# Half of the second Gram matrix taken in plain fp32 in the opening, with the opening's order and two bank queues changed

## The chip, the cores and the metric

The kernel runs on one NeuronCore of a Trainium2 chip. The metric is the time of one execution in microseconds (us). Before the change three runs gave 2222.56, 2222.73 and 2224.01 us, with 2222.73 as the median. One execution of the kernel was also profiled. All durations and waits below come from that trace.

The core's engines are called by the profile's names: PE (TensorE) multiplies matrices, ACT (ScalarE), DVE (VectorE) and POOL (GpSimd) do element-wise work, and SP issues the DMA transfers. Each engine works through its own queue in order, and they wait for each other by semaphores.

## What is computed

```python
def _attn_ref(q, k, v, tau):            # (4, 6080, 256) each
    qn = q / (norm(q, axis=1) + 1e-6);  kn = k / (norm(k, axis=1) + 1e-6)
    s = kn.transpose(0, 2, 1) @ qn / tau            # 256 x 256 per batch
    a = exp(s - s.max(-1));  a /= a.sum(-1) + 1e-9
    return v @ a
def _moe_ref(x, w_in, w_out):           # x: the 24320 rows of v @ a
    h = x @ w_in                                    # 2048 wide
    g = where(h >= 1, h, where(h <= -1, 0, (h + 1)**2 / 4))
    return g @ w_out
```

## The kernel before

**Per batch.** The Gram matrix k^T q (256 x 256) and the column norms give the softmax matrix. The kernel never forms v @ a: it multiplies the softmax matrix into each 256-wide slice of w_in (`make_W`) and applies the result to v.

**Groups.** The main loop runs over 192 groups: 4 batches, 6 column pairs of the transposed v (five of 2 x 512 columns, one of 2 x 480) and 8 slices. A group's 2 x 2 block product is done with seven block products instead of eight (Strassen's scheme in Winograd's form): `make_V` prepares the seven combinations of v (`V_T1` to `V_T4`, `V_11`, `V_21`, `V_22`) once per pair, `make_W` those of the weights. `h_ops` issues the seven products. They run through PSUM bank A (bank_119 in the order's rows), one of two Z banks (bank_125 or bank_126) and bank B (bank_120): products `S1*V_T1`, then `A11*V_11` (Z), `S2*V_T2` (Z), `A12*V_21` (A), `S3*V_T3` (Z), `S4*V_22` (B), `A22*V_T4` (Z). ACT and DVE copy and add between banks in between (L615, L617, L620, L624). `tile_ops` turns the four blocks of h into g (L589 to L599), and `o_ops` multiplies by w_out into four banks O00 to O11 (bank_121 to bank_124).

**Number format.** Each product of this kind is three fp32r matmuls (`mm3`, L378) on a value split into a high part and a remainder: high x high, high x remainder, remainder x high. A value is split by a cast (on ACT, or for two of the four g blocks on DVE, by `CAST_ON_DVE`) and a subtraction on DVE. The weights w_in and w_out arrive as float64 words and are converted by seven DVE instructions and two ACT instructions each (`convert`, L331 to L347).

**Gram matrices.** Batch 0's is done in the opening in plain fp32 from 1 MB chunks of k and q (L691), in four slots of memory that the g and v buffers take over afterwards; there ACT squares and DVE adds the squares for the norms (L682, L684). Batches 1 to 3 have theirs done during the groups of the batch before, in 24 chunks of 256 rows each (`gram_chunk`): a load, an ACT cast (L387), a DVE subtraction (L388), 12 matmuls (L378, `kqs`), and a DVE addition (L405).

**What sets the order.** Every operation is recorded with an engine, an estimated duration, a due number and its buffers. `Order.run` places them one after the other: on each engine, of what could start by its own clock, the one that starts first, and among those that could start now the one with the smallest due number. The order of placing is the order of each engine's queue on the chip; at run time only semaphores hold an instruction. A buffer pool gives a slot to whichever operation asks first, unless it is `ordered`. Bank A and bank B are pools of one slot each, so two groups that compete for bank A are served in the order in which the planner placed them.

## Time and profile before

| | us |
|---|---|
| three runs: median (lowest, highest) | 2222.73 (2222.56, 2224.01) |
| profiled execution | 2220.52 |
| its span, first to last instruction | 2218.7 |
| PE busy | 2168.8 |
| DVE busy | 1755.6 |
| ACT busy | 1655.3 |
| POOL busy | 219.2 |

The span is 1.8 us shorter than the execution it belongs to, and that execution is 2.2 us below the median of the runs. A row of the stretch view gives, for a stretch of the span, each engine's busy time with the number of instructions, then the clock granted to PE (1.00 is full speed), the share of the DMA engines' time in use, and GB/s. A row of the time line gives start, duration, engine, line, operation, operands, count of merged instructions, and in brackets the idle time before it and what ended it.

### The profile page before, as it was taken

How to read it: one execution, taken by the hardware profiler on the slowest of the kernel's cores; microseconds unless marked ns; L12 is line 12 of the kernel's file. 1: busy time of each engine (PE TensorE's matmuls, PEld its weight loads, DVE VectorE, ACT ScalarE, POOL GpSimd, SP SyncE). 2: the span in 40 equal slices, each digit the busy share in tenths (PEclk: the TensorE clock that was granted, in tenths of full speed). 3: DMA queues.
4: the chain of work that ended last, by engine and by line, in shares of the span. 5: the costliest groups of instructions: out<-in, count | busy, mean ns of one | idle time of the engine just before them, and what ended most of it. 6: DMA issues, size and time to landing. Idle time of an engine off the chain costs nothing.

```text
span 2218.7 us, 28354 instructions
## 1 busy us (share of the span) xinstructions
PE 2168.8 (98%) x10122; PEld 1818.8 (82%) x10122; DVE 1755.6 (79%) x2844; ACT 1655.3 (75%) x2964; POOL 219.2 (10%) x236
## 2 busy tenths in 40 slices
PE   8698999999999999999999999999999999999998
PEld 6476888888888888888888888888888888888887
DVE  7896778778878787877878888788787777778776
ACT  6576777777777777777778778787777777677775
POOL 1220000001012000010012100000002201000000
PEclk9799999999999999999999999999999999999999
DMA  8463444543435445445334554454442423333331
GB/s 329 164 223 111 171 178 143 193 159 136 150 124 203 172 145 187 156 152 196 114 112 177 185 187 145 160 197 146 165 148 90 175 102 115 126 104 118 120 119 35
DMA packets 84207, 340.16 MB, mean 153 GB/s; under 512 B 8800, under 2 KB 12896, under 8 KB 82656
## 3 DMA queue, kind: packets, MB, share of 16 engines
q1 hardware_dynamic: 84064, 338.33, 42.9%
q8 instruction: 80, 1.31, 0.2%
q14 instruction: 63, 0.52, 0.1%
HBM read 279.84 MB, written 58.46 MB: 152 GB/s over the span
## 4 chain that ended last, share of the span: by engine, by line
PE 91%; ACT 1%; DVE 1%; DMA 0%; issue 0%; POOL 0%; SPq 0%; ACTq 0%; POOLq 0%; DVEq 0%
PE bank L378 91%; ACT u L589 0%; DMA raw<-vT 0%; ACT u L591 0%; DVE u L593 0%; DVE x L599 0%; DVE w_mem L513 0%; ACT bank L617 0%; ACT mh_mem L615 0%; DVE bank L620 0%; DMA outT<-y_mem 0%; ACT v L552 0%; POOL sf_mem L510 0%; ACT x L598 0%; DVE mh_mem L624 0%
## 5 line engine op out<-in xcount | busy, mean ns | idle before, releaser
L378 PE MATMUL bank<-x,wout 128*128 128x512 f32 (+1 forms) x3972 | 1019.6, 389 | 2.3 <-DVE x L599 2.0
L378 PE MATMUL bank<-v,w_mem 128*128 128x512 f32 (+1 forms) x3264 | 850.7, 390 | 15.7 <-ACT bank L617 5.8
L378 PEld LDWEIGHTS bank<-x,wout 128*128 128x128 f32 x3972 | 741.4, 188 | 148.7 <-DVE x L599 5.1
L378 PEld LDWEIGHTS bank<-v,w_mem 128*128 128x128 f32 x3264 | 611.6, 189 | 147.5 <-ACT bank L617 8.9
L589 ACT ACTIVATE u<-bank 128x512 f32<-128x512 f32 (+1 forms) x576 | 342.1, 594 | 311.1 <-PE bank L378 300.4
L593 DVE TENSOR_TENSOR u<-bank,u 128x512 f32<-128x512 f32 (+1 forms) x576 | 391.7, 680 | 138.9 <-ACT u L591 138.6
L599 DVE TENSOR_TENSOR x<-u,x 128x512 fp32r<-128x512 f32 (+1 forms) x662 | 452.4, 691 | 28.4 <-ACT x L598 22.6
L591 ACT ACTIVATE u<-u 128x512 f32<-128x512 f32 (+1 forms) x768 | 468.0, 625 | 5.3
L598 ACT CAST x<-u 128x512 fp32r<-128x512 f32 (+1 forms) x331 | 202.6, 612 | 30.5 <-DVE u L593 27.8
L378 PE MATMUL bank<-x,w_mem 128*128 128x512 f32 (+1 forms) x768 | 208.6, 389 | 0.8 <-ACT bank L617 0.7
L620 DVE TENSOR_TENSOR bank<-bank,mh_mem 128x512 f32<-128x512 f32 (+1 forms) x192 | 133.0, 693 | 74.8 <-PE bank L378 73.3
L378 PE MATMUL bank<-g,wout 128*128 128x512 f32 (+1 forms) x636 | 177.7, 388 | 0.0
L593 DVE TENSOR_TENSOR u<-mh_mem,u 128x512 f32<-128x512 f32 (+1 forms) x192 | 135.6, 706 | 45.7 <-ACT u L591 45.6
L378 PEld LDWEIGHTS bank<-x,w_mem 128*128 128x128 f32 x768 | 143.8, 188 | 30.7 <-ACT bank L617 1.1
L624 DVE TENSOR_TENSOR mh_mem<-bank,mh_mem 128x512 f32<-128x512 f32 (+1 forms) x192 | 131.3, 684 | 39.9 <-PE bank L378 36.2
L615 ACT COPY mh_mem<-bank 128x512 f32<-128x512 f32 (+1 forms) x192 | 111.6, 581 | 51.3 <-PE bank L378 43.1
L596 DVE CAST x<-u 128x512 fp32r<-128x512 f32 (+1 forms) x331 | 141.5, 428 | 8.1
L378 PEld LDWEIGHTS bank<-g,wout 128*128 128x128 f32 x636 | 118.8, 188 | 23.7 <-DVE g L599 0.4
L617 ACT COPY bank<-bank 128x512 f32<-128x512 f32 (+1 forms) x192 | 109.9, 572 | 31.3 <-PE bank L378 22.0
L546 POOL TENSOR_TENSOR t<-raw,raw 128x512 f32<-128x512 f32 (+1 forms) x24 | 35.1, 1464 | 924.9 <-DMA raw<-vT 606.3
L589 ACT ACTIVATE u<-mh_mem 128x512 f32<-128x512 f32 (+1 forms) x192 | 119.2, 621 | 9.2 <-DVE mh_mem L624 8.6
L378 PEld LDWEIGHTS bank<-kqs 128*128 128x128 f32 (+1 forms) x864 | 113.2, 191 | 5.6
(83 smaller groups left out, 1491.8 us busy)
## 6 DMA issues: line engine op xcount, KB each, us to landing
w_mem<-w_d SPq DMA_DIRECT2D x160, 896.0 KB, 4.6
raw<-kq SPq DMA_DIRECT2D x69, 512.0 KB, 5.4
raw<-kqT SPq DMA_DIRECT2D x60, 512.0 KB, 6.1
w_d<-w_mem SPq DMA_DIRECT2D x32, 896.0 KB, 4.5
raw<-vT SPq DMA_DIRECT2D x40, 512.0 KB, 6.4
outT<-y_mem SPq DMA_DIRECT2D x80, 256.0 KB, 2.2
win<-win_d SPq DMA_DIRECT2D x24, 512.0 KB, 3.9
kq<-kq SPq DMA_DIRECT2D x11, 1024.0 KB, 8.3
```

What stands on the lines that cost most here:

```text
L378: nc.tensor.matmul(out, lhsT=lhs(a), rhs=rhs(c), start=start and m == 0, stop=stop and m == 2, skip_group_check=skip)
L546: op("POOL", pool_us(n), lambda: nc.gpsimd.tensor_tensor(out=tt(x), in0=a(), in1=c(), op=ALU.subtract), r=r, w=[ts[x]], due=due + d, gates ...
L589: op("ACT", act_us(n), lambda: nc.scalar.activation(us(), src(), IDENTITY_SAT240, scale=240.0), r=[h], w=[u], due=d_sat)
L591: op("ACT", act_us(n), lambda: nc.scalar.activation(us(), us(), AF.Square, bias=0.5, scale=1.0 / 480.0), w=[u], due=d_sq)
L593: op("DVE", dve_us(n), lambda: nc.vector.tensor_tensor(out=us(), in0=src(), in1=us(), op=ALU.max), r=[h], w=[u], due=d_max)
L596: op("DVE", dve1_us(n), lambda: nc.vector.tensor_copy(t.ap[:, 0, :n], us()), r=[u], w=[t], due=d_hi)
L598: op("ACT", act_us(n), lambda: nc.scalar.copy(t.ap[:, 0, :n], us()), r=[u], w=[t], due=d_hi)
L599: op("DVE", dve_us(n), lambda: nc.vector.tensor_tensor(out=t.ap[:, 1, :n], in0=us(), in1=f32(t.ap[:, 0, :n]), op=ALU.subtract), r=[u], w=[ ...
L615: op("ACT", act_us(n), lambda: nc.scalar.copy(m5.ap[:, :n], a.ap[:, :n]), r=[a], w=[m5], due=d - U)
L617: op("ACT", act_us(n), lambda: nc.scalar.copy(a.ap[:, :n], z.ap[:, :n]), r=[z], w=[a], due=d - U)
L620: op("DVE", dve_us(n), lambda: nc.vector.tensor_tensor(out=bb.ap[:, :n], in0=z.ap[:, :n], in1=m5.ap[:, :n], op=ALU.add), r=[z, m5], w=[bb] ...
L624: op("DVE", dve_us(n), lambda: nc.vector.tensor_tensor(out=h22.ap[:, :n], in0=z.ap[:, :n], in1=m5.ap[:, :n], op=ALU.add), r=[z, m5], w=[h2 ...
```

## The change

What it does, part by part:

- **Batch 1's first 3072 rows** (`EARLY` = 6 chunks of 512) are loaded into the opening's four slots behind batch 0's, and multiplied in plain fp32 into bank O11 (bank_124), with due number 8; DVE copies the sum once into batch 1's accumulator (L743). The 12 `gram_chunk` calls for these rows go. The other 12 are spread over groups 6 to 40 of batch 0 instead of 2 to 40. The squares for batch 1's norms are still all made during batch 0's groups.
- **The opening's order.** Due numbers for the opening are written as times; the softmax of batch 0 and the first `make_W` are `URGENT`, and an urgent operation may be preferred though it is up to `SOON` = 0.6 us from being ready. All eight w_out conversions are placed by the table at the end of the diff. The fold of the two halves of the squares (L701) is done by PE as a second matmul for each norm; the single matmul that writes bank B once (L699) moves behind the norms. The negated row maximum is made for each half of the softmax separately.
- **The first group's weights**: the four sums of `make_W` on DVE instead of POOL, and the split in two parts of three and four products. The order of the weights' parts is permuted.
- **Banks A and B** are ordered pools: groups get them in the order of their numbers.
- **Casts** of g blocks from group 8 on, and of v from the third column pair on, may go to ACT or DVE, whichever the planner finds first; in groups 0 to 7 all go to ACT.
- The planner's estimates of POOL's durations and of DMA bandwidth are changed.

```diff
+URGENT = -1000.0
+SOON = 0.6
...
-    BYTES = 350e3
+    BYTES = 380e3
...
-    def op(self, eng, dur, fn, r=(), w=(), due=0.0, gates=(), size=0):
+    def op(self, eng, dur, fn, r=(), w=(), due=0.0, gates=(), size=0, other=None):
...
+        o.alts = {eng: (dur, fn)}
+        if other:
+            o.alts[other[0]] = other[1:]
...
-                    if best is not None and t > now and t >= best[0][0]:
+                    t = base[o.n, e]
+                    if best is not None and t > now + SOON and t >= best[0][0]:
...
-                    key = (now, o.due, o.n) if t <= now else (t, o.due, o.n)
+                    key = (now, o.due, o.n) if t <= now or o.due <= URGENT and t <= now + SOON else (t, o.due, o.n)
                     if best is None or key < best[0]:
-                        best = (key, o)
+                        best = (key, o, e)
...
-            (t, _, _), o = pick
-            avail[o.eng].remove(o)
+            (t, _, _), o, o.eng = pick
+            t = max([t, base[o.n, o.eng]] + [self.slot(b, o.eng)[0] for b in o.bufs if b.ap is None])
+            o.dur, o.fn = o.alts[o.eng]
...
-A11, A12, A22, S1, S2, S3, S4, A21 = range(8)
+    return 0.35 + 0.0021 * n
...
+S1, A11, S2, A12, S3, S4, A22, A21 = range(8)
...
-CAST_ON_DVE = {(1, 0), (1, 1)}
...
+EARLY = 6
+FIRST = 8
...
     for i, n in enumerate(("A", "B", "O00", "O01", "O10", "O11")):
-        pools[n] = Pool([banks[i]])
+        pools[n] = Pool([banks[i]], ordered=n in ("A", "B"))
...
-        op("DVE", 0.1, lambda: V.tensor_scalar(out=nmax(), in0=nmax(), scalar1=-1.0, scalar2=None, op0=ALU.mult),
-           w=[c], due=due + 6)
+            op("DVE", 0.1, lambda it=it: V.tensor_scalar(out=nmax()[:, it:it + 1], in0=nmax()[:, it:it + 1],
+                                                        scalar1=-1.0, scalar2=None, op0=ALU.mult), w=[c],
+               due=due + 4 + it)
...
+    def make_W(b, i, due, gates=(), parts=((0, NS),), eng="POOL"):
...
-            op("POOL", pool_us(128), lambda d=d, a=a, c=c, o=o: nc.gpsimd.tensor_tensor(
+            v = {"POOL": nc.gpsimd, "DVE": nc.vector}[eng]
+            op(eng, pool_us(128) if eng == "POOL" else dve_us(128), lambda d=d, a=a, c=c, o=o, v=v: v.tensor_tensor(
                 out=f.ap[:, d, :], in0=f.ap[:, a, :], in1=f.ap[:, c, :], op=o), w=[f], due=due + 3)
-        op("ACT", act_us(NS * P), lambda: nc.scalar.copy(w.ap[:, 0], f.ap[:, :NS, :]), r=[f], w=[w], due=due + 5)
-        op("DVE", dve_us(NS * P), lambda: nc.vector.tensor_tensor(
-            out=w.ap[:, 1], in0=f.ap[:, :NS, :], in1=f32(w.ap[:, 0]), op=ALU.subtract), r=[f], w=[w], due=due + 7)
+        for j0, j1 in parts:
+            js, n = slice(j0, j1), (j1 - j0) * P
+            op("ACT", act_us(n), lambda js=js: nc.scalar.copy(w.ap[:, 0, js], f.ap[:, js, :]), r=[f], w=[w],
+               due=due + 5)
+            op("DVE", dve_us(n), lambda js=js: nc.vector.tensor_tensor(
+                out=w.ap[:, 1, js], in0=f.ap[:, js, :], in1=f32(w.ap[:, 0, js]), op=ALU.subtract), r=[f], w=[w],
+               due=due + 7)
...
             op("ACT", act_us(n), lambda: nc.scalar.copy(vs[x].ap[:, 0, :n], get()), r=r, w=[vs[x]], due=due + d,
-               gates=gates)
+               gates=gates, other=("DVE", dve1_us(n), lambda: nc.vector.tensor_copy(vs[x].ap[:, 0, :n], get()))
+               if (b, k) > (0, 1) else None)
...
-        if (x, y) in CAST_ON_DVE:
-            op("DVE", dve1_us(n), lambda: nc.vector.tensor_copy(t.ap[:, 0, :n], us()), r=[u], w=[t], due=d_hi)
-        else:
-            op("ACT", act_us(n), lambda: nc.scalar.copy(t.ap[:, 0, :n], us()), r=[u], w=[t], due=d_hi)
+        op("ACT", act_us(n), lambda: nc.scalar.copy(t.ap[:, 0, :n], us()), r=[u], w=[t], due=d_hi,
+           other=("DVE", dve1_us(n), lambda: nc.vector.tensor_copy(t.ap[:, 0, :n], us())) if g >= FIRST else None)
...
-    S = -120.0
+    T0 = 58.0
+    at = lambda us: (us - T0) / 0.65
...
+    n0 = len(big)
+    big += [(1, i * 512, P, 4) for i in range(EARLY)]
+    st.g = buf("Z")
+    g1 = buf("O11")
+    acc = Buf(acc_early)
...
+    def big_chunk(i, b, r0, p, T):
+        rb, g = Buf(kq_early), (st.g, g1)[b]
+        due = at(3.6 * i + 4) if b == 0 else 8.0
+        kq_ops.append(load(rb, lambda: kq[b, r0:r0 + p * T].rearrange("(p t) s c -> p (t s c)", t=T),
+                           lambda: rb.ap[:p, :T * 512], due - 25 if b == 0 else at(56), p * T * 2048,
+                           [kq_ops[n0 - 1]] if b else ()))
+        last = i == (n0 if b == 0 else len(big)) - 1
+        for t in range(T):
+            def mm(t=t):
+                for it in range(CT):
+                    k0 = t * 512 + it * P
+                    nc.tensor.matmul(g.ap[:, it * C:(it + 1) * C], lhsT=rb.ap[:p, k0:k0 + P],
+                                     rhs=rb.ap[:p, t * 512 + C:t * 512 + 2 * C], start=(r0 == 0 and t == 0 and it == 0),
+                                     stop=(last and t == T - 1 and it == CT - 1), skip_group_check=True)
+            op("PE", CT * 0.433, mm, r=[rb], w=[g], due=due)
+        if b:
+            return
...
-        def mm(rb=rb, p=p, T=T, i=i):
-            for t in range(T):
-                for it in range(CT):
-                    k0 = t * 512 + it * P
-                    nc.tensor.matmul(st.g.ap[:, it * C:(it + 1) * C], lhsT=rb.ap[:p, k0:k0 + P],
-                                     rhs=rb.ap[:p, t * 512 + C:t * 512 + 2 * C],
-                                     start=(i == 0 and t == 0 and it == 0),
-                                     stop=(i == len(big) - 1 and t == T - 1 and it == CT - 1), skip_group_check=True)
-        op("PE", T * CT * 0.45, mm, r=[rb], w=[st.g], due=due)
...
-            op("PE", 1.0, lambda rb=rb: nc.tensor.matmul(banks[1], lhsT=ident, rhs=rb.ap[:, :TB], start=True, stop=True),
-               r=[rb], w=[buf("B")], due=due)
-    op("DVE", dve_us(512), lambda: nc.vector.tensor_tensor(out=accv()[:, :512], in0=accv()[:, :512],
-                                                          in1=accv()[:, 512:1024], op=ALU.add), w=[acc0], due=-60)
...
     def norm_sums():
         for j in range(2 * CT):
-            nc.tensor.matmul(st.pt.ap[:, j:j + 1], lhsT=accv()[:, j * P:(j + 1) * P], rhs=ones[:, 0:1], start=True,
-                             stop=True)
-    op("PE", 1.0, norm_sums, r=[acc0], w=[st.pt], due=-60)
-    softmax(0, -50)
-    for i, due in enumerate((-110, -60, -30)):
-        make_w_in(i, due, [kq_ops[min(2 + 4 * i, 12)]])
-    for i, due in enumerate((-80, -50, -20, -10, 0)):
-        make_w_out(i, due, [kq_ops[min(5 + 4 * i, 12)]])
-    make_V(0, 0, -40, [kq_ops[9]], 1.0)
+            for h in range(2):
+                nc.tensor.matmul(st.pt.ap[:, j:j + 1], lhsT=acc.ap[:, h * 512 + j * P:h * 512 + (j + 1) * P],
+                                 rhs=ones[:, 0:1], start=(h == 0), stop=(h == 1))
+    def mark_b():
+        nc.tensor.matmul(banks[1], lhsT=ident, rhs=acc.ap[:, :TB], start=True, stop=True)
+    for i, x in enumerate(big):
+        big_chunk(i, *x)
+    st.pt = buf("Z")
+    op("PE", 1.4, norm_sums, r=[acc], w=[st.pt], due=URGENT - 20)
+    op("PE", 0.9, mark_b, r=[acc], w=[buf("B")], due=at(56))
+    softmax(0, URGENT - 20)
+    sts[1].g = buf("gacc")
+    op("DVE", dve_us(512), lambda: nc.vector.tensor_copy(sts[1].g.ap.rearrange("p i c -> p (i c)"), g1.ap), r=[g1],
+       w=[sts[1].g], due=10.0)
+    for kind, i, due, gate_ in (("in", 0, 14, 1), ("out", 0, 26, 3), ("in", 1, 34, 5), ("v", 0, 38, 7), ("out", 1, 46, 9),
+                                ("in", 2, 54, 11), ("out", 2, 60, 12), ("out", 3, 70, 12), ("out", 4, 84, 12),
+                                ("out", 5, 94, 12), ("out", 6, 104, 12), ("out", 7, 114, 12)):
+        if kind == "v":
+            make_V(0, 0, at(due), [kq_ops[gate_]], 2.0)
+        else:
+            (make_w_in if kind == "in" else make_w_out)(i, at(due), [kq_ops[gate_]])
...
-            make_W(0, i, d - 20, gate(g - 3))
+            make_W(0, i, URGENT - 10 if i == 0 else d - 20, gate(g - 3), *((((0, 3), (3, NS)), "DVE") if i == 0 else ()))
...
-        if g + 5 < FP:
-            make_w_out(g + 5, d + 4, gate(g))
...
-            lo_, hi_ = 2, KP * FP - 8
-            span = hi_ - lo_
+            rows = range(EARLY * 512 if b == 0 else 0, N, 256)
+            lo_, hi_ = (6 if b == 0 else 2), KP * FP - 8
+            for c, r0 in enumerate(rows):
+                if q == lo_ + c * (hi_ - lo_) // len(rows):
+                    gram_chunk(b + 1, r0, min(P, (N - r0) // RT), d + 8, gate(g))
             for c in range(24):
-                if q == lo_ + c * span // 24:
-                    r0 = c * 256
-                    p = min(P, (N - r0) // RT)
-                    gram_chunk(b + 1, c, r0, p, d + 8, gate(g))
+                if q == (8 if b == 0 else 2) + c * (KP * FP - (16 if b == 0 else 10)) // 24:
                     s, r = divmod(c, 2 * NCW)
                     square_piece(b + 1, s, r // NCW, r % NCW, d + 16, gate(g))
```

The first place is PE's queue between the last matmul of batch 0's Gram matrix and the first product of group 0. Before (`mh_mem` holds the squares, `diag` the scales, `s` the softmax rows, `win` and `eT` the operands of `make_W`, `v` and `w_mem` those of the group):

```order
L691 MATMUL bank_125<-kq_0_78 128x256 x4
L707 MATMUL bank_126<-ones,mh_mem 128x1 x4
L452 MATMUL bank_126<-diag,ones 128x128 x2
L474 MATMUL bank_126<-ident,s 128x128 x4
L378 MATMUL bank_125<-win_109,eT 128x256 x12
L378 MATMUL bank_126<-win_110,eT 128x256 x12
L378 MATMUL bank_125<-win_111,eT 128x256 x12
L378 MATMUL bank_119<-v_87,w_mem 128x512 x3
```

And in the changed kernel, the same place (bank_124 takes batch 1's sum):

```order
L709 MATMUL bank_124<-kq_1_79 128x256 x8
L729 MATMUL bank_126<-ones,mh_mem 128x1 x8
L734 MATMUL bank_120<-mh_mem,ident 128x512
L709 MATMUL bank_124<-kq_2_80 128x256 x4
L469 MATMUL bank_126<-diag,ones 128x128 x2
L709 MATMUL bank_124<-kq_2_80 128x256 x4
L709 MATMUL bank_124<-kq_3_81 128x256 x8
L492 MATMUL bank_126<-ident,s 128x128 x4
L709 MATMUL bank_124<-kq_0_78 128x256 x4
L395 MATMUL bank_125<-win_109,eT 128x256 x12
L395 MATMUL bank_126<-win_110,eT 128x256 x12
L709 MATMUL bank_124<-kq_0_78 128x256 x4
```

Behind these rows stand 8 more fp32 matmuls of batch 1 and then group 0; the last 8 of the 48 stand between group 0's products, and the third weight product has moved behind group 1's. So 40 fp32 matmuls now stand between the steps of the softmax, two weight products before group 0 instead of three.

The second place is DVE's queue in the same stage, from the scales to the negated maximum. Before, with rows of the weight conversion (L332 to L347) between the rows of the softmax:

```order
L445 TENSOR_SCALAR diag<-ident,cols_117 128x128
L345 TENSOR_SCALAR u_103<-u_103 128x512
L341 SCALAR_TENSOR_TENSOR u_104<-raw_101,u_104 128x512
L455 COPY rq<-bank_126 128x256
L347 SCALAR_TENSOR_TENSOR win_111<-u_107,u_103 128x512
L458 SCALAR_TENSOR_TENSOR s<-bank_125,cols_117,rq 128x256
L334 TENSOR_SCALAR u_107<-raw_101 128x512
L461 TENSOR_REDUCE cols_117<-s 128x1
L338 SCALAR_TENSOR_TENSOR u_107<-raw_101,u_107 128x512
L458 SCALAR_TENSOR_TENSOR s<-bank_125,cols_117,rq 128x256
L345 TENSOR_SCALAR u_104<-u_104 128x512
L461 TENSOR_REDUCE cols_117<-s 128x1
```

And in the changed kernel:

```order
L462 TENSOR_SCALAR diag<-ident,cols_117 128x128 x2
L355 SCALAR_TENSOR_TENSOR u_104<-raw_99,u_104 128x512
L472 COPY rq<-bank_126 128x256
L475 SCALAR_TENSOR_TENSOR s<-bank_125,cols_117,rq 128x256
L478 TENSOR_REDUCE cols_117<-s 128x1
L480 TENSOR_SCALAR cols_117<-cols_117 128x1
L475 SCALAR_TENSOR_TENSOR s<-bank_125,cols_117,rq 128x256
```

The conversion rows have moved out from between the softmax rows; they stand behind them.

The third place is PE's queue where the first column pair ends: group 7 is its last group, group 8 the first of the second pair. The operand v_94 is group 8's `V_T1`; v_87 in bank_119 is group 7's `V_T1`, and the buffer v_87 is afterwards used again for group 8's `V_T3`. Before:

```order
L378 MATMUL bank_119<-v_94,w_mem 128x512 x3
L378 MATMUL bank_125<-x_1010,w_mem 128x512 x3
L378 MATMUL bank_121<-x_661,wout 128x512 x3
L378 MATMUL bank_122<-x_661,wout 128x512 x3
L378 MATMUL bank_125<-x_1010,w_mem 128x512 x3
L378 MATMUL bank_126<-v_88,w_mem 128x512 x3
...
L378 MATMUL bank_119<-v_88,w_mem 128x512 x3
L378 MATMUL bank_119<-v_87,w_mem 128x512 x3
L378 MATMUL bank_125<-v_87,w_mem 128x512 x3
```

And in the changed kernel, from group 7's `V_T1` on:

```order
L395 MATMUL bank_119<-v_87,w_mem 128x512 x3
L395 MATMUL bank_121<-g_86,wout 128x512 x3
...
L395 MATMUL bank_126<-v_93,w_mem 128x512 x3
L395 MATMUL bank_119<-v_94,w_mem 128x512 x3
L395 MATMUL bank_125<-x_1029,w_mem 128x512 x3
L395 MATMUL bank_121<-x_658,wout 128x512 x3
...
L395 MATMUL bank_119<-v_88,w_mem 128x512 x3
L395 MATMUL bank_126<-x_1029,w_mem 128x512 x3
L395 MATMUL bank_125<-v_87,w_mem 128x512 x3
```

Before, group 8 took bank A ahead of group 7, and the two rows with v_87 stood next to each other; now group 7 comes first, and between its use of v_87 and group 8's stand 23 rows.

More of the change, by code (lines that the diff above doesn't have):

```diff
@@ L46, in __init__ @@
         self.all = all
+URGENT = -1000.0
+SOON = 0.6
 class Op:
-    __slots__ = ("eng", "dur", "fn", "due", "deps", "gates", "bufs", "next", "count", "start", "end", "n", "size")
+    __slots__ = ("eng", "dur", "fn", "due", "deps", "gates", "bufs", "next", "count", "start", "end", "n", "size",
+                 "alts")
 class Order:
@@ L125, in open_ @@
         def open_(o):
-            t = self.ready_at(o, o.deps)
-            for g in o.gates:
-                t = max(t, g.start)
-            base[o.n] = t
-            avail[o.eng].append(o)
+            for e in o.alts:
+                t = self.ready_at(e, o.deps)
+                for g in o.gates:
+                    t = max(t, g.start)
+                base[o.n, e] = t
+                avail[e].append(o)
         for o in self.ops:
@@ L379, in mm3, with gram_chunk @@
                              skip_group_check=skip)
-    def gram_chunk(b, i, r0, p, due, gates):
+    def gram_chunk(b, r0, p, due, gates):
         st = sts[b]
@@ L488, in channel_attention_moe @@
     w_buf = {}
-    def make_W(b, i, due, gates=()):
+    def make_W(b, i, due, gates=(), parts=((0, NS),), eng="POOL"):
         st = sts[b]
@@ L664, in channel_attention_moe @@
         p = min(P, (N - r0) // T)
[L665 removed]
+        big.append((0, r0, p, T))
         r0 += p * T
[L667 to L675 removed]
+    n0 = len(big)
@@ L676, in channel_attention_moe @@
         for t in range(0, T, 2):
+            src = lambda t=t: rb.ap[:p, t * 512:t * 512 + 1024]
             if i == 0:
-                op("ACT", act_us(1024), lambda rb=rb: nc.scalar.activation(accv()[:, :1024], rb.ap[:, :1024],
-                                                                          AF.Square), r=[rb], w=[acc0], due=due)
+                op("ACT", act_us(1024), lambda src=src: nc.scalar.activation(acc.ap, src(), AF.Square), r=[rb], w=[acc], due=due)
                 continue
@@ L696, in channel_attention_moe @@
[L696 to L703 removed]
+            op("ACT", act_us(1024), lambda sq=sq, src=src: nc.scalar.activation(sq.ap[:p], src(), AF.Square), r=[rb], w=[sq], due=due)
@@ L705, in norm_sums @@
+            op("DVE", dve_us(1024), lambda sq=sq: nc.vector.tensor_tensor(
+                out=acc.ap[:p], in0=acc.ap[:p], in1=sq.ap[:p], op=ALU.add), r=[sq], w=[acc], due=due)
     def norm_sums():
         for j in range(2 * CT):
-            nc.tensor.matmul(st.pt.ap[:, j:j + 1], lhsT=accv()[:, j * P:(j + 1) * P], rhs=ones[:, 0:1], start=True,
-                             stop=True)
-    op("PE", 1.0, norm_sums, r=[acc0], w=[st.pt], due=-60)
-    softmax(0, -50)
-    for i, due in enumerate((-110, -60, -30)):
-        make_w_in(i, due, [kq_ops[min(2 + 4 * i, 12)]])
```

41 lines of the change are left out of this document (13 added, 28 removed).

## The prediction

> **What bounds the kernel now.** I read the page first, then PE's stretches, then PE's time line where a stretch is not full. The page gives the span, the busy shares and, in forty slices, PE's busy share and the clock granted to it:
>
> ```profile
> span 2218.7 us, 28354 instructions
> PE 2168.8 (98%) x10122; PEld 1818.8 (82%) x10122; DVE 1755.6 (79%) x2844; ACT 1655.3 (75%) x2964; POOL 219.2 (10%) x236
> PE   8698999999999999999999999999999999999998
> PEclk9799999999999999999999999999999999999999
> ```
>
> PE is busy for 98% of the span, and only the first slices are not full. So a change can win in two ways alone: fewer matmuls, or less idle and slow-clock time in the opening. The stretch view cuts the span there:
>
> ```profile
> 10.70:42.40 31.70, 31.70 (x145) 27.58 (x143) 29.42 (x41) 20.76 (x24) 0.00 (x0) 1.00 1.01 392
> 53.70:58.20 4.50, 0.00 (x0) 0.00 (x0) 4.50 (x7) 3.03 (x5) 0.00 (x0) 0.76 0.00 0
> 58.20:82.36 24.16, 11.91 (x52) 10.40 (x53) 21.36 (x51) 8.31 (x16) 5.96 (x6) 0.55 0.24 88
> 82.36:130.00 47.64, 36.53 (x143) 25.24 (x144) 43.63 (x77) 37.37 (x66) 9.73 (x16) 0.96 0.62 221
> 130.00:189.50 59.50, 58.79 (x293) 48.68 (x293) 52.35 (x79) 42.63 (x76) 12.71 (x15) 1.00 0.55 197
> 189.50:216.00 26.50, 19.69 (x68) 12.62 (x68) 15.96 (x26) 16.88 (x30) 1.27 (x1) 0.81 0.30 109
> 216.00:2213.00 1997.00, 1995.65 (x9376) 1683.34 (x9374) 1577.29 (x2555) 1513.84 (x2734) 182.23 (x187) 1.00 0.42 147
> ```
>
> From 216 us on PE idles 1.35 us in 1997: that part is worth what its matmuls take. Before it there are three poor stretches: the softmax (53.7 to 82.36), the first groups (82.36 to 130, with DVE 92% busy), and 189.5 to 216.
>
> **Unit prices.** Three rows of PE's time line and their successors give the spacing, and the page's group of fp32 matmuls its count:
>
> ```profile
> 10.73 31.72 PE L691 MATMUL bank<-kq 128*128 128x256 f32 x144
> 132.41 0.84 PE L378 MATMUL bank<-v,w_mem 128*128 128x512 f32 x3
> 133.09 0.84 PE L378 MATMUL bank<-x,wout 128*128 128x512 f32 x3
> 134.45 1.60 PE L378 MATMUL bank<-kqs 128*128 128x256 f32 x12
> 135.89 2.23 PE L378 MATMUL bank<-x,wout 128*128 128x512 f32 x9
> 137.95 1.60 PE L378 MATMUL bank<-win,eT 128*128 128x256 f32 x12
> 139.39 0.86 PE L378 MATMUL bank<-v,w_mem 128*128 128x512 f32 x3
> ...
> L691 PE MATMUL bank<-kq 128*128 128x256 f32 (+1 forms) x192 | 44.7, 395 | 7.5 <-DMA kq<-kq 7.5
> ```
>
> A product of three 512-wide matmuls takes 0.68 us (132.41 to 133.09), a Gram chunk 1.44 us (134.45 to 135.89), a weight product 1.44 us (137.95 to 139.39). The program writes 96 matmuls at L691 and the trace has 192, so each plain fp32 matmul is two records of 31.72 / 144 = 0.220 us: 0.441 us, and 3.52 us for the eight of a 512-row chunk.
>
> **The removed matmuls.** Twelve chunks of 1.44 us are 17.3 us. PE was full where they stood, so this comes off nearly one to one. By the queues, three of them stood before the twelfth product into bank B, and nine behind it. I use that product as a common point, because both queues have 492 512-wide matmuls between group 0's first product and it. In the trace it is the second half of this row, at 242.53 us:
>
> ```profile
> 241.85 1.52 PE L378 MATMUL bank<-v,w_mem 128*128 128x512 f32 x6
> ```
>
> Behind it the queues differ by the nine chunks alone: **-13.0 us**. The loads, casts and subtractions of the chunks go too, but there they stood beside a full PE and count nothing.
>
> **The added fp32 matmuls.** 48 of 0.441 us are 21.2 us, more than the 17.3 they replace. They pay only because 40 of them stand in the softmax stage:
>
> ```profile
> 58.21 1.87 PE L707 MATMUL bank<-ones,mh_mem 128*128 128x1 f32 x8 [4.53 <-DVE mh_mem L701]
> 64.17 1.33 PE L452 MATMUL bank<-diag,ones 128*128 128x128 f32 x4 [4.09 <-DVE diag L445]
> 70.63 1.18 PE L474 MATMUL bank<-ident,s 128*128 128x128 f32 x4 [5.14 <-ACT s L466]
> 73.33 0.80 PE L378 MATMUL bank<-win,eT 128*128 128x256 f32 x2 [1.52 <-ACT eT L480]
> 74.47 6.73 PE L378 MATMUL bank<-win,eT 128*128 128x256 f32 x34 [0.34 <-DVE eT L481]
> 82.36 0.73 PE L378 MATMUL bank<-v,w_mem 128*128 128x512 f32 x2 [1.16 <-ACT w_mem L512]
> ...
> 78.44 2.89 POOL L510 TENSOR_TENSOR sf_mem<-sf_mem 128x128 f32<-128x128 f32 x4 [16.46 <-ACT sf_mem L505]
> ```
>
> PE waits here four times, and what it does runs at a clock of 0.55. The new queue from 53.7 on, at full clock: a chunk 3.5; norms, now 16 records of at most 0.23 (1.87 / 8), I take half, 1.9; the write of bank B, 0.9; four fp32 1.8; scales 0.7; twelve fp32 5.3; transposes 0.6; four fp32 1.8; two weight products 2.9; twelve fp32 5.3. Sum 24.7, or 78.4 us with no wait. Waits remain: for the last addition of squares (about 1; it ended near 57 before), for the scales (about 1.4: the chain took 4 us from DVE's copy of the norms, and only 2.7 us of matmuls cover it) and for eT (about 1). That puts group 0 at **81.5 us instead of 82.36**, bounded by 79 and 86. The softmax's own chain is shorter than before (no conversions between its DVE rows, no fold, the four POOL sums of 2.89 us on DVE), but PE's queue is now the later of the two, so little of that shows. The DMA has room: the six chunks are 6.3 MB, 16 us at 392 GB/s, and 53.7 to 58.2 moved nothing before.
>
> [...]
>
> The rows for the waits that are new:
>
> ```profile
> 100.51 1.83 PE L378 MATMUL bank<-g,wout 128*128 128x512 f32 x6
> ...
> L405 DVE TENSOR_TENSOR gacc<-bank,gacc 128x512 f32<-128x512 f32 x69 | 47.7, 692 | 57.9 <-PE bank L378 57.7
> ```
>
> They are priced at nothing, with this cover. Six of the seven g buffers lie in the chunks' memory, so group 0's casts wait for the last fp32 matmul; that one stands between group 0's third and fourth product, before any cast can be due. DVE's copy of bank O11 (about 0.69, as the addition at L405 takes) must come before group 0's first w_out product into that bank; before, the first w_out product came at 100.51, 18 us after group 0's start. On SP the six loads stand ahead of most w_out loads; two w_out slices are converted before the softmax, and the next is needed a group later. If these covers fail, each microsecond of lateness is one on PE.
>
> **The first groups.** From 82.36 to 242.53 PE had 492 / 3 x 0.68 + 11 x 1.44 = 127.4 us of work and took 160.2: 32.8 lost. The same sum for each stretch gives 17.8 lost by 130 us, 2.0 by 189.5, and 12.4 in 189.5 to 216.
>
> ```profile
> 189.54 0.84 PE L378 MATMUL bank<-v,w_mem 128*128 128x512 f32 x3
> 192.46 1.55 PE L378 MATMUL bank<-v,w_mem 128*128 128x512 f32 x3 [2.07 <-DVE u L593]
> 194.71 1.95 PE L378 MATMUL bank<-v,w_mem 128*128 128x512 f32 x3 [0.71 <-ACT v L552]
> 199.08 5.16 PE L378 MATMUL bank<-v,w_mem 128*128 128x512 f32 x12 [2.42 <-ACT bank L617]
> ...
> L513 DVE TENSOR_TENSOR w_mem<-sf_mem,w_mem 128x896 fp32r<-128x896 f32 x32 | 35.0, 1093 | 14.8 <-ACT w_mem L512 14.5
> L388 DVE TENSOR_TENSOR kqs<-raw,kqs 128x1024 fp32r<-128x1024 f32 x72 | 87.7, 1219 | 3.1 <-ACT kqs L387 3.0
> L596 DVE CAST x<-u 128x512 fp32r<-128x512 f32 (+1 forms) x331 | 141.5, 428 | 8.1
> L341 DVE SCALAR_TENSOR_TENSOR u<-raw,u 128x512 uint32<-128x512 uint32 x16 | 11.5, 716 | 0.0
> L332 DVE TENSOR_SCALAR u<-u 128x512 f32<-128x512 f32 x16 | 7.0, 436 | 0.2 <-ACT u L331 0.2
> ```
>
> The last loss is an order that could not run: group 8 had bank A before group 7, and its `V_T3` needed the buffer that group 7's late first product still read; so PE, ACT, DVE and PE followed each other with no w_out product left to fill. With ordered banks 23 rows lie between the two uses. I take 12.4 down to 2.
>
> The first loss stays. DVE bounds it, and from group 0's weight remainder to group 3's sum into bank B, DVE's queue now holds eight conversion instructions more (0.436 to 0.716 us each, about 4.5 us), but four casts (0.428), one Gram subtraction (1.219) and two weight remainders (1.093) fewer, 5.1 us: equal. I take 15 lost there, since some of the 3.5 us of leftover fp32 matmuls and the moved weight product fall into its holes. New work to the common point: 492 / 3 x 0.68 + 3.5 + 6 x 1.44 + 3 x 1.44 = 128.0; plus 15 and 2 is 145. From 81.5 the common point comes at 226.5 instead of 242.5: **-16.0 us**.
>
> **The sum.** -16.0 - 13.0 = -29.0 on the span: 2189.7; the profiled execution would be 2220.5 - 29 = 2191.5, and the median 2222.7 - 29 = 2193.7, say **2194 us**. The tail and the other batches count nothing: the rows above leave 1.35 us to win or lose there by waits.
>
> **The rivals.** (1) *The stall at the pair's turn stays*, because v's four POOL sums and casts, not the bank order, are late. For it speaks that PE did wait for ACT's v at 194.71; against it, that this wait came after the late product. It gives 10 us back: 2204. (2) *The first groups gain too*: with casts off DVE and no Gram chunks there, the loss falls to 7: 2186, or lower with an earlier group 0. (3) *The fill holds the softmax*: PE takes its queue in order, so a chunk that lands late, or the half clock, delays the transposes one for one. At half clock the queue of 24.7 us takes twice that, and about 3 of its waits vanish: group 0 comes 22 us later, 2216. Against it: the DMA's empty stretch and the full clock of 10.7 to 42.4 for the same kind of matmul. (4) *Slower: DVE becomes late in every group.* By the queues 108 casts move to DVE (46 us) and 12 chunks' subtractions and additions leave (about 23): 23 us net on 1577 in the long stretch, 79% to 80%. If in-order DVE then releases PE late, each of some 184 groups pays; the gain is gone at 29 / 184 = 0.16 us a group, and at 0.3 us the time is 2249. Against it stand the 420 us of DVE idle there.
>
> [...]
>
> ```profile
> 44.63 3.79 POOL L546 TENSOR_TENSOR t<-raw,raw 128x512 f32<-128x512 f32 x1 [43.18 <-DMA raw<-vT]
> 48.51 1.27 POOL L546 TENSOR_TENSOR t<-raw,t 128x512 f32<-128x512 f32 x1
> ```
>
> The same subtraction took 3.79 and 1.27 us. [...]
>
> **Chances and range.** Forecast (2186 to 2202) 0.58; (1), up to 2212, 0.22; (2), below 2186, 0.11; (3) 0.04; (4) 0.05, of which 0.03 is slower. What one can tell from no change is about 0.2%, 4.4 us. So faster 0.94, same 0.03, slower 0.03. The range reaches over most of (1) and half of (2): 2182 to 2210.
>
> **What would show it.** The stretch from 53.7 to group 0 should show PE nearly full at clock 1.00 and group 0 near 81.5; if group 0 comes past 86, the fill was mispriced. Around 180 to 200 us no wait of PE over 1 us should be left; if it is, (1) holds. From 82 to 130 PE should still wait for DVE. PE's idle time beyond 216 us should stay below 5 us; if it passes 20, (4) holds. If the span falls by 13 us only, the opening gave nothing.

## The result, and the profile after

Four runs gave 2183.39 to 2186.23 us, with 2184.93 as the median; the kernel before gave 2223.37 beside them. The ratio is 0.983 (95% interval 0.981 to 0.984): 38.4 us on the medians. The profiled executions went from 2220.52 to 2184.81 us and their spans from 2218.7 to 2183.0, 35.7 us. The forecast was 2194 us, with 2182 to 2210 as the range; 2184.93 lies inside it, but below the 2186 to 2202 us that the prediction held most likely.

The page of the changed kernel, the same rows as before the change:

```profile
span 2183.0 us, 28082 instructions
PE 2158.9 (99%) x10082; PEld 1815.8 (83%) x10082; DVE 1778.7 (81%) x2937; ACT 1592.5 (73%) x2845; POOL 213.3 (10%) x232
PE   8899999999999999999999999999999999999999
PEclk9999999999999999999999999999999999999999
```

PE's second slice, which holds the softmax stage and the first groups (54.6 to 109 us), is 8 instead of 6, its clock digit 9 instead of 7, and DVE has taken over work from ACT. The stretch view, cut at group 0's start (78.41 us) and at PE's end (2178.76):

```profile
53.70:60.00 6.30, 4.29 (x26) 3.28 (x25) 4.91 (x10) 1.76 (x3) 1.14 (x1) 0.98 0.95 362
60.00:82.00 22.00, 22.00 (x111) 19.43 (x110) 18.52 (x46) 10.34 (x21) 2.92 (x4) 0.93 0.78 288
78.41:130.00 51.59, 42.87 (x190) 34.16 (x189) 45.95 (x79) 37.42 (x67) 10.56 (x16) 0.93 0.44 153
...
189.50:216.00 26.50, 26.50 (x124) 22.06 (x123) 22.12 (x38) 20.41 (x38) 0.00 (x0) 1.00 0.53 175
216.00:2178.76 1962.76, 1961.86 (x9178) 1652.39 (x9176) 1591.73 (x2638) 1437.43 (x2585) 177.31 (x187) 1.00 0.42 147
```

From 60 us on the softmax stage is full, the stretch with the stall (189.5 to 216) is full, and beyond it 0.9 us are idle. What is left stands between 78 and 165 us, as PE's list of waits shows (total, times, longest); ahead of it are only the loads and one wait before the norms (L729). The first five of the list's eight rows, of which the other three are 0.9 us (DVE's addition at L646), 0.8 us (DVE's Gram subtraction at L405, beyond 216 us) and 0.2 us (DVE's subtraction at L621):

```profile
PE bank L709 <- DMA kq<-kq: 6.6, 3, 5.4
PE bank L395 <- DVE u L617: 3.9, 1, 3.9
PE bank L395 <- ACT bank L639: 3.3, 3, 1.7
PE bank L395 <- DVE bank L642: 2.0, 2, 1.0
PE bank L729 <- DVE mh_mem L723: 2.0, 1, 2.0
```

PE's time line through the filled stage (L709 is the plain fp32 matmul of both batches), and the first products after it:

```profile
34.34 16.40 PE L709 MATMUL bank<-kq 128*128 128x256 f32 x72 [1.08 <-DMA kq<-kq]
50.91 3.72 PE L709 MATMUL bank<-kq 128*128 128x256 f32 x16 [0.17 <-DMA kq<-kq]
56.63 1.92 PE L729 MATMUL bank<-ones,mh_mem 128*128 128x1 f32 x16 [2.00 <-DVE mh_mem L723]
59.35 3.28 PE L709 MATMUL bank<-kq 128*128 128x256 f32 x8
...
78.41 1.73 PE L395 MATMUL bank<-v,w_mem 128*128 128x512 f32 x6
93.06 1.03 PE L395 MATMUL bank<-v,w_mem 128*128 128x512 f32 x3 [3.89 <-DVE u L617]
221.37 1.55 PE L395 MATMUL bank<-v,w_mem 128*128 128x512 f32 x6
```

Batch 0's Gram matrix ends at 50.74 us, PE waits 0.17 us for a load and 2.00 us for the last addition of squares, and group 0 starts at 78.41. The common point, the second half of the last row, comes at 222.05 instead of 242.53: -20.5 us, where -16.0 was forecast.

### The profile page after: what moved, and what is told of

Same layout as the page of the kernel before. It is cut to its first block, busy times and chain, and to the rows that moved or that the text cites. A ratio compares the mean times of both kernels' runs of the same rounds, so it can differ in the third digit from the quotient of the medians.

```text
span 2183.0 us, 28082 instructions
## 1 busy us (share of the span) xinstructions
PE 2158.9 (99%) x10082; PEld 1815.8 (83%) x10082; DVE 1778.7 (81%) x2937; ACT 1592.5 (73%) x2845; POOL 213.3 (10%) x232
## 4 chain that ended last, share of the span: by engine, by line
PE 94%; DVE 3%; DMA 1%; issue 1%; ACT 1%; POOL 0%; SPq 0%; DVEq 0%; ACTq 0%; POOLq 0%
PE bank L395 92%; PE bank L709 1%; DMA kq<-kq 1%; DVE mh_mem L723 1%; DVE u L617 0%; DMA raw<-kq 0%; POOL sf_mem L529 0%; DVE x L621 0%; DVE u L355 0%; DVE u L358 0%; DVE u L362 0%; DVE win L364 0%; DVE w_mem L535 0%; ACT u L613 0%; DVE mh_mem L646 0%
## 5 line engine op out<-in xcount | busy, mean ns | idle before, releaser
L621 DVE TENSOR_TENSOR x<-u,x 128x512 fp32r<-128x512 f32 (+1 forms) x658 | 453.4, 696 | 22.6 <-ACT x L619 18.7
L619 ACT CAST x<-u 128x512 fp32r<-128x512 f32 (+1 forms) x306 | 187.3, 614 | 79.4 <-DVE u L617 79.3
L395 PE MATMUL bank<-g,wout 128*128 128x512 f32 (+1 forms) x660 | 183.7, 388 | 0.2 <-DVE g L621 0.2
L620 DVE CAST x<-u 128x512 fp32r<-128x512 f32 (+1 forms) x352 | 151.4, 436 | 9.2
L646 DVE TENSOR_TENSOR mh_mem<-bank,mh_mem 128x512 f32<-128x512 f32 (+1 forms) x192 | 131.3, 684 | 33.3 <-PE bank L395 28.6
L395 PEld LDWEIGHTS bank<-g,wout 128*128 128x128 f32 x660 | 123.3, 188 | 24.7 <-DVE g L621 0.6
L569 POOL TENSOR_TENSOR t<-raw,t 128x512 f32<-128x512 f32 (+1 forms) x48 | 67.6, 1407 | 476.9 <-DVE v L578 378.7
```

What stands on the lines that cost most here:

```text
L395: nc.tensor.matmul(out, lhsT=lhs(a), rhs=rhs(c), start=start and m == 0, stop=stop and m == 2, skip_group_check=skip)
L569: op("POOL", pool_us(n), lambda: nc.gpsimd.tensor_tensor(out=tt(x), in0=a(), in1=c(), op=ALU.subtract), r=r, w=[ts[x]], due=due + d, gates ...
L619: op("ACT", act_us(n), lambda: nc.scalar.copy(t.ap[:, 0, :n], us()), r=[u], w=[t], due=d_hi, other=("DVE", dve1_us(n), lambda: nc.vector.t ...
L620: other=("DVE", dve1_us(n), lambda: nc.vector.tensor_copy(t.ap[:, 0, :n], us())) if g >= FIRST else None)
L621: op("DVE", dve_us(n), lambda: nc.vector.tensor_tensor(out=t.ap[:, 1, :n], in0=us(), in1=f32(t.ap[:, 0, :n]), op=ALU.subtract), r=[u], w=[ ...
L646: op("DVE", dve_us(n), lambda: nc.vector.tensor_tensor(out=h22.ap[:, :n], in0=z.ap[:, :n], in1=m5.ap[:, :n], op=ALU.add), r=[z, m5], w=[h2 ...
```

## The experiments

All times are medians of four runs; the kernel before gave 2223.12, 2223.37 and 2222.24 us beside the first, second and third four.

**1. The order of the banks.** Taken out of the changed kernel (`e1_unordered`):

```diff
-        pools[n] = Pool([banks[i]], ordered=n in ("A", "B"))
+        pools[n] = Pool([banks[i]], ordered=False)
```

> The changed kernel with banks A and B given to whoever asks first, as before the change. The rule of the ordered banks is what removed the stall at the pair's turn: it comes back, PE waits some 10 us between 189 and 216 us, and the time is 2195 us (+10). Rival: with the new due numbers and casts the planner takes group 7 before group 8 by itself (in this kernel's PE queue it does), so the rule has no work left to do here: no wait of PE over 1 us between 180 and 200 us and 2183 to 2187 us.

2198.54 us, +13.6, where the theory had +10. The kind of place is the theory's, the place itself is not: at batch 0's turn from the first to the second column pair the queue stays as in the changed kernel, as the rival had it, but at the same turn of batch 3 PE's queue again has the later group's use of bank A (group 152) ahead of the earlier one's (group 151; v_94, then v_93):

```
L395 MATMUL bank_119<-v_94,w_mem 128x512 x3
L395 MATMUL bank_119<-v_93,w_mem 128x512 x3
```

There the time line shows the stall of before with its three waits:

```profile
1767.73 0.96 PE L395 MATMUL bank<-v,w_mem 128*128 128x512 f32 x3 [2.07 <-DVE u L617]
1769.40 0.50 PE L395 MATMUL bank<-v,w_mem 128*128 128x512 f32 x1 [0.71 <-ACT v L575]
1773.53 5.15 PE L395 MATMUL bank<-x,w_mem 128*128 128x512 f32 x12 [2.42 <-ACT bank L639]
...
1800.15 5.28 PE L395 MATMUL bank<-x,wout 128*128 128x512 f32 x15 [2.48 <-ACT y_mem L672]
```

2.07, 0.71 and 2.42 us are to the hundredth the waits at 192.46, 194.71 and 199.08 before the change. So the stall is a property of the order, and it can fall on another batch's turn. It is not the whole of the 13.6 us: the last row is a further wait, for ACT's copy of an output bank, with a slow clock behind it (0.97 over 1800 to 1850 us; the 15 matmuls of that row took 5.28 us, 15 others at 1791.39 3.56). Whether that wait comes from the bank order too is not shown.

The opposite edit, the ordered banks alone in the kernel before (`e2_before_ordered`):

```diff
-        pools[n] = Pool([banks[i]])
+        pools[n] = Pool([banks[i]], ordered=n in ("A", "B"))
```

> The kernel before with ordered banks A and B and nothing else of the change. The order of the banks alone caused the 12.4 us lost between 189.5 and 216 us: at most 2 are left, and the time is 2213 us (-10), group 0 still at 82.4 us. Rival: the lateness of v's sums and casts caused it, or the wait reappears in another place: 2221 to 2225 us, with ACT's v or DVE's u before PE's products of group 8.

2212.34 us, -10.8; -7.4 between the profiled executions. The stretch of the stall, then, from PE's time line, the opening and a new wait:

```profile
189.50:216.00 26.50, 24.81 (x117) 20.52 (x116) 21.65 (x35) 22.98 (x42) 1.29 (x1) 1.00 0.55 192
```

```profile
10.51 40.04 PE L691 MATMUL bank<-kq 128*128 128x256 f32 x184
...
80.60 0.73 PE L378 MATMUL bank<-v,w_mem 128*128 128x512 f32 x2 [2.25 <-ACT w_mem L512]
...
130.34 0.80 PE L378 MATMUL bank<-x,wout 128*128 128x512 f32 x1 [2.64 <-ACT x L598]
```

6.8 us of idle time there have become 1.7, at full clock; a wait of 2.64 us in another place takes part of it back. The opening is that of the kernel before, and yet its Gram matrix ends at 50.55 us, not 53.68, and group 0 starts at 80.60, not at the expected 82.4. Between 20 and 30 us the DMA moved 407 GB/s here and 349 in the kernel before. So the late end is no mark of that code; from one execution each, which is usual can't be told. It also means that 1.8 of the 7.4 us between the two traces stand at group 0 already, and are not the bank order's: that leaves 5.6 us for it by the traces, for 10.8 by the medians.

**2. The fill.** No chunk of batch 1 in the opening (`e3_early0`), three (`early3`), and nine (`early9`) instead of six:

```diff
-EARLY = 6
+EARLY = 0
```

With none, the copy of bank O11's sum is left out too; it would have nothing to copy.

> The changed kernel without the fp32 chunks of batch 1 in the opening: all 24 chunks are done during batch 0's groups again. The fill of the softmax stage is what pays: 17.3 us of chunks come back, the 3.5 us of fp32 matmuls that stood behind group 0 go, and group 0 starts by the softmax's own chain, 75 to 78 us, at a granted clock near 0.5 before it: 2185 + 17.3 - 3.5 - (0 to 3) = 2196 to 2199 us. Rival: the shorter softmax chain and the reordered opening gave most of the gain, the 48 matmuls cost what they save: 2184 to 2189 us, group 0 at 72 us or before. Other rival: without the fill the slow clock holds the first groups too: above 2202 us.

> The changed kernel with three chunks of batch 1 in plain fp32 instead of six. Theory: a chunk that fits the softmax stage is worth its 2.88 us of Gram matmuls nearly whole; three chunks of fp32 fewer leave that stage part empty and group 0 at 76 to 78 us, as without any: the three chunks given back cost 8.6 us less up to 2.5 us, 2191 to 2194 us. Rival: most of the gain needs the stage full to its end, since the slow clock returns in the part left empty: 2195 us or more.

> The changed kernel with nine chunks of 512 rows of batch 1 in plain fp32 instead of six. By the prices of the prediction three chunks save 8.6 us of Gram matmuls and cost 10.6 us of fp32 matmuls, which the softmax stage has no more room for: 2185 + 2 = 2187 us. Rival: the 13 us in which PE waits between 82 and 145 us take part of them: 2177 to 2182 us. Other rival: batch 1's sum in bank O11 comes later than the w_out product that needs that bank, and group 0 stalls: above 2190 us.

| chunks | us | against the row above |
|---|---|---|
| 0 | 2199.52 | |
| 3 | 2193.65 | -5.9 |
| 6 | 2184.93 | -8.7 |
| 9 | 2183.65 | -1.3 |

The run without any ended 0.5 us above its theory's range, the one with three inside its theory's. Six chunks are worth 14.6 us; the prices of the prediction give 17.3 - 3.5 = 13.8. Without any, group 0 starts at 78.01 us behind seven waits of PE; with them at 78.41. The 40 matmuls in the stage are 17.6 us of work and move group 0 by 0.4 us, though the plan without them also has three weight products ahead of group 0 instead of two. Two rows of `e3_early0`:

```profile
56.77 3.54 PE L729 MATMUL bank<-ones,mh_mem 128*128 128x1 f32 x16 [5.89 <-DVE mh_mem L723]
78.01 1.55 PE L395 MATMUL bank<-v,w_mem 128*128 128x512 f32 x6
```

The stretch from 53.7 to 216 us with 0, 3, 6 and 9 chunks:

```profile
53.70:216.00 162.30, 140.69 (x643) 112.35 (x644) 146.11 (x251) 122.52 (x223) 27.65 (x33) 0.94 0.47 167
```

```profile
53.70:216.00 162.30, 145.92 (x661) 117.75 (x660) 141.40 (x246) 120.10 (x219) 28.33 (x33) 0.95 0.47 169
```

```profile
53.70:216.00 162.30, 150.06 (x703) 123.78 (x702) 142.93 (x248) 119.09 (x218) 27.34 (x33) 0.97 0.52 186
```

```profile
53.70:216.00 162.30, 153.92 (x725) 126.82 (x724) 137.90 (x239) 116.46 (x213) 26.63 (x33) 0.99 0.57 201
```

PE's idle time there falls from 21.6 to 16.4, 12.2 and 8.4 us, and the clock rises: the first three chunks fill holes but hardly raise the clock (0.94 to 0.95), the next three raise it to 0.97. The last three fell between theory and rival: their 24 matmuls stand behind group 0's start, in waits of the first groups, and what they win there pays for the 10.6 - 8.6 = 2.0 us of net work and little more: its runs (2182.95 to 2183.83 us) overlap with the changed kernel's.

**3. The casts.** All fixed as before (`e4_fixed_casts`); fixed in groups 0 to 7 alone (`first_dve`); fixed from group 8 on alone, and v's on ACT (`late_fixed`). The core of the last; in the first the condition is only `x == 1`, in the second it is `g < FIRST and x == 1`, with the two removed lines as the other branch:

```diff
-        op("ACT", act_us(n), lambda: nc.scalar.copy(t.ap[:, 0, :n], us()), r=[u], w=[t], due=d_hi,
-           other=("DVE", dve1_us(n), lambda: nc.vector.tensor_copy(t.ap[:, 0, :n], us())) if g >= FIRST else None)
+        if g >= FIRST and x == 1:
+            op("DVE", dve1_us(n), lambda: nc.vector.tensor_copy(t.ap[:, 0, :n], us()), r=[u], w=[t], due=d_hi)
+        else:
+            op("ACT", act_us(n), lambda: nc.scalar.copy(t.ap[:, 0, :n], us()), r=[u], w=[t], due=d_hi)
```

> The changed kernel with the casts of g fixed as before (two of the four blocks on DVE, two on ACT, in groups 0 to 7 too) and those of v on ACT. The free choice of engine is worth nothing where PE never waits for it: 2184 to 2189 us, of which up to 3 us because four to six casts of 0.43 us go back to DVE in the first groups, where PE waits for DVE. Rival: the free casts gave the part of the gain that the prediction didn't have (some 7 us): 2190 to 2194 us.

> The changed kernel with the casts of two of the four g blocks on DVE again in groups 0 to 7 only; from group 8 on the free choice stays. The kernel with all casts fixed lost 11.6 us. Theory: about half of that was lost in the first groups, where DVE is busy 90% and each cast put back delays the copies and subtractions that PE waits for: 2189 to 2193 us, with PE's new waits before 160 us. Rival: the first groups lose nothing, the free choice later is what pays: 2184 to 2187 us.

> The changed kernel with casts in groups 0 to 7 all on ACT as in it, but fixed to two blocks on ACT and two on DVE from group 8 on, and v's casts on ACT. Theory: only the two waits of 1.95 us seen beyond 216 us with all casts fixed belong to the later groups: 2187 to 2190 us. Rival: the free choice later carries all of the 11.6 us: 2194 to 2198 us.

2196.53, 2191.27 and 2193.18 us: +11.6, +6.3 and +8.2. The first lies beyond theory and rival, the second is the theory's, the third lies between its two. In the first groups the casts that went back to DVE show after 130 us; the changed kernel, then `first_dve`:

```profile
130.00:160.00 30.00, 28.80 (x142) 23.84 (x142) 30.00 (x45) 25.54 (x48) 14.09 (x15) 1.00 0.61 214
```

```profile
130.00:160.00 30.00, 26.73 (x120) 21.89 (x119) 26.54 (x41) 20.07 (x38) 11.57 (x11) 0.89 0.40 142
```

PE is idle for 3.3 us there instead of 1.2, and the clock falls to 0.89. Beyond 216 us `late_fixed` has two equal waits for ACT's copy of a bank (L640):

```profile
709.97 2.00 PE L395 MATMUL bank<-v,w_mem 128*128 128x512 f32 x6 [1.97 <-ACT bank L640]
711.77 1.48 PE L395 MATMUL bank<-x,wout 128*128 128x512 f32 x3
...
1248.49 1.66 PE L395 MATMUL bank<-v,w_mem 128*128 128x512 f32 x6 [1.97 <-ACT bank L640]
1249.98 0.86 PE L395 MATMUL bank<-x,wout 128*128 128x512 f32 x3
```

On ACT that copy stands behind a cast of a g block, at the end of a run of ACT without a pause in which two casts of v stand too (the second is the first row):

```profile
704.30 0.62 ACT L575 CAST v<-t 128x512 fp32r<-128x512 f32 x1
...
708.81 0.63 ACT L621 CAST x<-u 128x512 fp32r<-128x512 f32 x1
709.33 0.59 ACT L640 COPY bank<-bank 128x512 f32<-128x512 f32 x1
```

Behind the first wait a product of three matmuls took 1.48 us instead of 0.86: the clock was halved (0.50 over 712 to 714 us; behind the second wait it was 1.00 over 1248 to 1252). With 3.8 us more idle time than the changed kernel beyond 216 and 1.7 us lost to the clock (an estimate, half of 3.4 us at a clock of 0.50), 5.5 of the 8.2 us are seen there.

The edit fixes two kinds of cast at once. In the changed kernel's trace DVE makes 417 casts of g blocks, for 384 before, and 75 of v's 168, for none before: of the 108 casts that moved to DVE, most are v's. Which of the two kinds the 8.2 us belong to was not tried.

Since any edit makes the planner place everything anew, the changed kernel and `late_fixed` were planned again with another estimate of DMA bandwidth (`plan390`, `late_plan390`):

```diff
-    BYTES = 380e3
+    BYTES = 390e3
```

> The changed kernel planned anew: only the planner's estimate of DMA bandwidth goes from 380e3 to 390e3, which gives another order of the same instructions on every engine. Theory: a stall such as the two waits of 1.97 us with fixed casts comes from how one plan falls out, and any new plan moves the time by several us: PE's idle time beyond 216 us differs from 0.9 us by 2 or more, and the time from 2185 by 3 to 8 us. Rival: with free casts and ordered banks a plan hardly matters: 2182 to 2187 us, at most 2 us idle beyond 216 us.

> The kernel with the casts fixed from group 8 on (2193.2 us, 4.7 us of PE's waits beyond 216 us), planned anew in the same way. Theory: fixed casts cost the later groups by themselves: again 4 us or more of waits beyond 216 us and 2190 to 2195 us. Rival: they cost nothing, as in the kernel before (1.35 us of waits there with fixed casts), and the two waits belonged to that one plan: under 2 us of waits beyond 216 us and 2184 to 2188 us.

2186.82 and 2194.91 us: the rival for the first, the theory for the second. The stretch beyond 216 us of `plan390`, then of `late_plan390`:

```profile
216.00:2170.00 1954.00, 1953.71 (x9138) 1645.10 (x9137) 1599.40 (x2636) 1435.83 (x2574) 175.23 (x187) 1.00 0.42 148
```

```profile
216.00:2170.00 1954.00, 1949.04 (x9095) 1639.13 (x9094) 1545.39 (x2500) 1487.54 (x2687) 179.13 (x187) 1.00 0.42 148
```

The new plan alone costs 1.9 us. The free casts are worth 8.1 us in it, as 8.2 in the other: 4.7 us of idle time, and the two waits of `late_fixed` stand in this plan too, now both with the half clock behind them (0.66 over 712 to 716 us, 0.58 over 1252 to 1256; 2.55 and 1.90 us for six matmuls that took 1.66 at 1248.49 in `late_fixed`):

```profile
712.83 2.55 PE L395 MATMUL bank<-v,w_mem 128*128 128x512 f32 x6 [1.97 <-ACT bank L640]
...
1251.37 1.90 PE L395 MATMUL bank<-v,w_mem 128*128 128x512 f32 x6 [1.97 <-ACT bank L640]
```

So these waits go with the fixed casts, not with one plan. They need not come in every order: the kernel before had fixed casts and was idle for 1.35 us beyond 216. Why it was spared is open.

**4. The wait before the norms.** Four of batch 1's matmuls ahead of them (`cover`), and this with nine chunks (`cover9`):

```diff
-            op("PE", CT * 0.433, mm, r=[rb], w=[g], due=due)
+            op("PE", CT * 0.433, mm, r=[rb], w=[g], due=URGENT - 30 if i == n0 + 1 and t < 2 else due)
```

> The changed kernel with four of batch 1's fp32 matmuls moved ahead of the norms, into PE's wait of 2.0 us for the last addition of squares. Theory: that wait and the half clock seen behind it (0.50 from about 59.8 to 63.8 us) cost group 0 some 3 to 4 us: group 0 at 75 to 76 us, 2181 to 2183 us. Rival: the softmax's chain starts later and group 0 comes no earlier, or the first groups, bound by DVE, give the gain back: 2184 to 2186 us.

> The changed kernel with both edits that lowered the time a little: nine chunks in plain fp32, and four of the matmuls ahead of the norms. Theory: the two gains lie in different places, the waits of the first groups and the wait before the norms, and add to 1 to 4 us: 2181 to 2184 us. Rival: group 0 comes at 78 us whatever stands ahead of the norms, and the first groups are bound by DVE: 2184 to 2187 us.

2184.06 and 2180.29 us. The first is the rival's, and its runs (2183.04 to 2185.08 us) overlap with the changed kernel's: in `cover` the wait of 2.00 us and the half clock are gone (next rows; 1.00 over 60 to 82 us, for 0.93 in the changed kernel), the scales now wait 0.53, and group 0 comes at 78.57, because six more of the fp32 matmuls (2.6 us) now stand before it:

```profile
56.89 1.84 PE L729 MATMUL bank<-ones,mh_mem 128*128 128x1 f32 x16
59.53 1.89 PE L709 MATMUL bank<-kq 128*128 128x256 f32 x8
61.95 0.71 PE L469 MATMUL bank<-diag,ones 128*128 128x128 f32 x4 [0.53 <-DVE diag L462]
78.57 1.74 PE L395 MATMUL bank<-v,w_mem 128*128 128x512 f32 x6
```

With nine chunks the two edits together give 4.6 us, more than the 0.9 and 1.3 they gave alone and below the theory's range. The runs of `cover9`, 2179.94 to 2181.87 us, lie below all of the changed kernel's: the fastest version of this study. Its stage and first groups:

```profile
53.70:216.00 162.30, 154.81 (x735) 127.66 (x735) 138.24 (x243) 118.59 (x217) 26.97 (x33) 1.00 0.56 202
```

PE is idle for 7.5 us in this stretch, at full clock; the changed kernel was for 12.2 at 0.97.

## Why the prediction was right, point by point

By the profiled executions the forecast was -29.0 and the result -35.7 us. The 6.7 us are mis-sized terms: group 0's start 3.1, the first groups 1.4, what lies behind the common point 0.8 (-13.8 for -13.0), the time after PE's end 1.4 (4.24 us, before 5.66).

The time lies where rival 2 put it, below 2186 us with a chance of 0.11, but not for rival 2's reason: the first groups' loss did not fall to 7 us, it stayed at 15.6. What brought it there is group 0's earlier start, 3.1 us, with smaller terms.

- **Removed matmuls and their prices: right.** Beyond the common point PE's time fell by 13.8 us, nine chunks being 13.0 and the idle time 0.45; six fp32 chunks are worth 14.6 us, for 13.8.
- **Group 0's start: the sum was right, its starting point was not.** From the Gram matrix's end to group 0 it took 78.41 - 50.74 = 27.7 us, for 81.5 - 53.7 = 27.8. But 53.7 was one execution's: experiment 1 shows 50.55 with the same opening, and so group 0 came before the lower bound of 79. That the sum agrees to 0.1 us is partly luck. Its own terms, 24.7 of work and 3.4 of waits, give 81.8, not 81.5; the waits were 2.2 us, with none for the scales or for eT; and against that a stretch of 3.4 us ran at half clock (0.93 over 60 to 82 us), where full clock was forecast. That the filled stage keeps full clock was the author's estimate, and no run had shown it: over 60 to 82 us the clock was 0.90 to 1.00 in the runs with six or nine chunks, 0.92 with three, 0.66 with none.
- **The new waits at nothing: nothing contradicts it.** No wait of PE for a w_out slice, nor for bank O11's copy, shows among its waits.
- **The stall at the pair's turn: right, its price less sure.** 12.4 us down to 2 was forecast; that stretch is full now, and the two edits of the bank order moved the time by -10.8 (5.6 by the traces) and +13.6 (with a second wait in it). Ordered banks alone are enough to remove the stall from the kernel before; in the changed kernel that turn has no wait above 0.6 us without them either, and they keep the stall from another turn. Rival 1 falls.
- **The first groups' loss stays: right.** From 78.41 to 222.05 are 143.6 us for a forecast of 145; with 128.0 of work 15.6 are lost, and PE still waits for DVE (3.89 us at 93.06). It rests on the casts that left DVE there, which the working set against the conversions: `first_dve` loses 6.3 us without them.
- **The step that was wrong: the free casts as a risk.** Rival 4 saw them make DVE late in every group. DVE did go from 79% to 81% beyond 216 us, and its casts of g from 428 to 436 ns on average, but PE's idle time there went from 1.35 to 0.9: the choice works the other way. Fixing the casts costs 11.6 us. A likely way is that free casts keep out of the way of ACT's copies, as the waits with casts ahead of the copy suggest; with casts of g and v fixed together, it is argued and not shown. The forecast took the idle time beyond 216 us as given. With free casts it stayed below 1 us in both plans; with fixed casts it was near 5 in both.
- **Adding up.** Taken out one at a time, the fill is worth 14.6, the bank order 13.6 and the casts 11.6 us, together 39.8 for a gain of 38.4. Such parts need not add up: the two halves of the casts gave 6.3 + 8.2 = 14.5 for the 11.6 of both. So the sum doesn't tell what the reordered opening is worth, and it was not tried alone. Two traces without the fill give a hint: from the norms' first matmul to group 0 it took 78.01 - 56.77 = 21.2 us with it (`e3_early0`) and 80.60 - 56.46 = 24.1 with the opening of before (`e2_before_ordered`), at half clock for most of the way in both (0.66 and 0.65 over 60 to 82 us). The medians' gain is 2.7 us above the profiled one because the profiled execution of the kernel before was 2.85 us below its median; its runs lay between 2217 and 2225 us.

## What to carry to other kernels

Where a queue runs dry for a dependent chain, independent work of a worse price per unit pays nearly in full as long as it fits the hole, and pays little beyond its end: 2.4 us a chunk up to the sixth here, of the 2.9 it saves, and 0.4 after (1.3 with the wait before the norms covered). When resources are handed out in the order of asking, read the queue for a later user ahead of an earlier one whose data it needs; the same inversion brought the same three waits at another place of the plan. A choice of engine that looks neutral by busy shares is judged by what queues behind it, and a planner's edit is compared with a second plan before a few microseconds are put down to it.
